# Attention rows stored with g alone and their norms beside them; the readers multiply

## Chip, cores, metric

One core of a Trainium2 chip runs the whole program. The metric is the device time of one execution in microseconds (us).

## What is computed

```python
# attention, 8 batches, 8 heads, 576 rows, 64 columns a head
kv  = einsum('bhsd,bhse->bhde', k, v)
out = einsum('bhsd,bhde->bhse', q, kv)
x   = out / sqrt(mean(out * out, -1) + 1e-6) * g_norm      # -> x [4608, 512]
# one of 8 experts for each row whose skip score is above 0; the others pass
e   = argmax(x @ w_gate); p = softmax(x @ w_gate)[e]
x   = x + p * (maximum(x @ w1[e], 0) @ w2[e])              # 512 -> 1024 -> 512
# dense part, all rows
h   = x @ w_in                                             # 512 -> 2048
y   = (h * sigmoid(h)) @ w_out                             # 2048 -> 512
```

## The kernel before, in words

Three stages follow each other: attention with the routing of its rows (0 to about 138 us in the trace), the eight experts (147 to 418 us), the dense part (418 us to the end).

**Attention.** The loop runs over batches b = 0 to 7 and, inside, over units u of four heads and two 128-row tiles (u = 0 to 3); an odd batch has a fifth unit, the 64 rows left over of each of two batches (`attend_rest`). Tiles of one pair of batches are numbered 0 to 8, so a pair has 9 x 8 = 72 norms a partition. `attend` of a unit stands one unit behind the rest of the loop (`prev`). For each unit (`attend_main`, L448) TensorE writes po (L458) in PSUM, which holds for each head 64 output columns and 9 scores (the skip score and 8 gate logits, not yet normed). ScalarE squares the 64 columns into sq (L477) and copies them into the rows tile in SBUF (L484). VectorE copies the 9 scores into sc (L485) and sums the squares into ssq (L487). In two units of batch 6 ScalarE makes the sums itself (`sums_by_act`, L472). In batch 7 VectorE multiplies by g while it copies (`g_early`, L480).

`norm` (L601) takes ssq and makes inv, one over the root, with ten small VectorE operations (L607 to L627) on mh and tmp in SBUF, once for each batch and in two parts for batch 7. `scale` (L638) then multiplies each row tile on GpSimd, by inv and by g, two operations a tile; `scale_inv` does it for batch 7's last tiles on ScalarE (L653, eight operations) and VectorE (L648). `routing` works on sc times inv (L697) and gives each row its expert, its gate weight and its place.

`store` writes a batch's rows to `xs` in DRAM. A row there has 4 pieces of XQ = 129 floats: 128 columns and the gate weight. `STORES` says at which batch and unit each store is issued on SP's queue; batches 6 and 7 are stored behind the loop. `weave` puts the operations of several generators alternately into an engine's order; beside that the order is the order of the program text.

**Experts.** While expert u runs, the rows of expert u + 1 are gathered (L990, GpSimd's queue), three tiles of up to 128 rows, named xe_0 to xe_2. An expert has 8 steps f; a step is 12 matmuls into ph (`first`, L1325), the two halves of h by ScalarE (L1331) and VectorE (L1332), and 9 matmuls of the step before into acc (`second`, L1377). In the last steps of an expert TensorE transposes the next expert's rows into pt (L1226), and ScalarE and VectorE copy them as high and low halves xT (L1237, L1238). Weights arrive as f32 and are split into high and low halves: w by ScalarE and VectorE (L186, L187). Some pieces of the dense weights go through a longer split: five VectorE operations (L197 to L209), one of ScalarE, two GpSimd multiplies and subtractions (L221, L222), and a VectorE sum (L217) that waits for L222. Each engine takes its own instructions strictly in order.

**Dense part.** Groups of rows are read by place (`fetch_blocks`, L1024); for each tile VectorE transposes blocks (L1259, and L1288 in `operand_parts`) and the operands are made for TensorE.

## Time and profile before

| | |
|---|---|
| median of 3 runs (lowest to highest) | 1189.66 us (1189.15 to 1190.32) |
| the profiled execution, its own time | 1186.21 us |
| its span in the trace | 1184.4 us |
| mean granted TensorE clock | 0.962 of full speed |
| busy: TensorE, its weight loads, VectorE, ScalarE, GpSimd | 95%, 78%, 52%, 39%, 31% of the span |
| chain that ended last | PE 84%, DVE 7%, DMA 3%, issue 2%, ACT 1%, POOL 1% |
| costliest lines | TensorE L1377 278.7 us, L1325 269.4 us, L1520 265.1 us |

PE is TensorE, DVE VectorE, ACT ScalarE, POOL GpSimd, SP SyncE. A busy share over the whole span mixes the three stages; a stage has to be read from a window of its own. The chain goes back from the last instruction, at each step to what released it.

### The profile page before, as it was taken

To read this page: it belongs to the slowest core of one execution; us is meant where nothing else is said; L and a number is where in the kernel's file an instruction comes from. 1 tells how busy PE (TensorE), PEld (TensorE's weight loads), DVE (VectorE), ACT (ScalarE), POOL (GpSimd) and SP (SyncE) were. 2 spreads that over 40 slices of the span, in tenths; PEclk is the share of its full clock that TensorE was granted. 3 is DMA by queue.
4 is the path that set the end of the run, shared out by engine and by line. 5 is a ranking of instruction groups with operands and counts; after the bars stand their busy time and mean duration, and the time that the engine had idled before them with its cause. 6 is when DMAs were issued, how large, how long until landed. Compare 5 with 4: busy or idle time off the path is not lost.

```text
span 1184.4 us, 18142 instructions
## 1 busy us (share of the span) xinstructions
PE 1119.5 (95%) x6991; PEld 929.4 (78%) x6991; DVE 615.7 (52%) x1217; ACT 467.3 (39%) x877; POOL 361.8 (31%) x360
## 2 busy tenths in 40 slices
PE   7785299999999899999999999999999999999998
PEld 6674298888887788888888888888888888888886
DVE  2679867778788667643544622355222453223222
ACT  2444244444455433432433444433244432344221
POOL 2668435444444347233053324120043200000000
PEclk8787599999999899999999999999999999999999
DMA  9956656666766624058651376532566422654202
GB/s 337 358 227 254 213 174 204 207 203 201 218 219 220 214 85 156 1 180 282 202 157 56 129 267 211 180 125 85 192 214 217 145 107 103 218 186 173 103 36 71
DMA packets 65272, 211.16 MB, mean 178 GB/s; under 512 B 9840, under 2 KB 24688, under 8 KB 53024
## 3 DMA queue, kind: packets, MB, share of 16 engines
q1 hardware_dynamic: 55760, 189.44, 46.2%
q0 software_dynamic: 8064, 20.48, 5.9%
q8 instruction: 56, 0.92, 0.3%
q10 hardware_dynamic: 1360, 0.05, 0.1%
q14 instruction: 32, 0.26, 0.1%
HBM read 162.67 MB, written 47.27 MB: 177 GB/s over the span
## 4 chain that ended last, share of the span: by engine, by line
PE 84%; DVE 7%; DMA 3%; issue 2%; ACT 1%; POOL 1%; SPq 0%; POOLq 0%; ACTq 0%; another core or an unknown queue 0%; DVEq 0%
PE acc L1520 22%; PE acc L1377 19%; PE ph L1325 19%; PE pa L1473 11%; PE pc L1473 6%; PE pb L1473 3%; DMA v<-in_v_dram 1%; PE pt L1226 1%; PE kv L417 1%; PE po L458 1%; DVE ssq L487 1%; DVE w L187 1%; POOL x L222 0%; DVE scratch L699 0%; PE G L438 0%
## 5 line engine op out<-in xcount | busy, mean ns | idle before, releaser
L1377 PE MATMUL acc<-w,h 128*128 128x512 f32 x1128 | 278.7, 393 | 3.0 <-DVE xe L1387 1.8
L1325 PE MATMUL ph<-xT,w 128*128 128x512 f32 (+7 forms) x1344 | 269.4, 350 | 1.2 <-DVE w L187 1.2
L1520 PE MATMUL acc<-entry,h 128*128 128x512 f32 x1152 | 265.1, 392 | 0.0
L1520 PEld LDWEIGHTS acc<-entry,h 128*128 128x128 f32 x1152 | 216.3, 188 | 47.9
L1325 PEld LDWEIGHTS ph<-xT,w 128*128 128x128 f32 x1344 | 228.6, 192 | 31.1 <-DVE w L187 1.4
L1377 PEld LDWEIGHTS acc<-w,h 128*128 128x128 f32 x1128 | 202.1, 182 | 50.6 <-DVE xe L1387 2.1
L1024 POOL DMA_INDIRECT x<-xs,qidx x128 | 128.3, 1002 | 113.9 <-DVE room L1288 48.8
L1501 DVE TENSOR_TENSOR h<-g,h 128x512 fp32r<-128x512 f32 x96 | 66.5, 693 | 147.9 <-ACT h L1500 147.9
L1473 PE MATMUL pa<-b,entry 128*128 128x512 f32 x576 | 141.8, 393 | 0.0
L1473 PEld LDWEIGHTS pa<-b,entry 128*128 128x128 f32 x576 | 108.2, 188 | 24.8
L1500 ACT ACTIVATE h<-g 128x512 fp32r<-128x512 f32 x96 | 60.5, 630 | 146.6 <-PE acc L1520 146.6
L1339 DVE TENSOR_TENSOR h<-sg,h 128x512 fp32r<-128x512 f32 x48 | 34.8, 724 | 107.5 <-ACT h L1338 107.5
L187 DVE TENSOR_TENSOR w<-stg_None,w 128x1024 fp32r<-128x1024 f32 x64 | 80.2, 1255 | 17.9 <-ACT w L186 17.6
L1455 ACT ACTIVATE g<-g 128x512 f32<-128x512 f32 x72 | 45.4, 633 | 103.3 <-DVE g L1453 103.3
L1337 ACT ACTIVATE sg<-ph 128x512 f32<-128x512 f32 x48 | 28.6, 597 | 128.2 <-PE ph L1325 128.2
L221 POOL TENSOR_TENSOR x<-x,x 128x512 f32<-128x512 f32 x32 | 41.5, 1298 | 113.9 <-DVE x L209 109.1
L1473 PE MATMUL pc<-b,entry 128*128 128x512 f32 x288 | 74.3, 393 | 0.0
L1331 ACT ACTIVATE h<-ph 128x304 fp32r<-128x304 f32 (+6 forms) x64 | 27.9, 436 | 112.0 <-PE ph L1325 108.9
L186 ACT ACTIVATE w<-stg_None 128x1024 fp32r<-128x1024 f32 x64 | 67.1, 1050 | 9.0 <-DMA xs<-rows 8.6
L1473 PEld LDWEIGHTS pc<-b,entry 128*128 128x128 f32 x288 | 54.1, 188 | 12.4
L222 POOL TENSOR_TENSOR x<-x,w 128x512 f32<-128x512 f32 x32 | 62.9, 1967 | 0.8 <-ACT w L220 0.8
L1453 DVE TENSOR_TENSOR g<-pc,u 128x512 f32<-128x512 f32 x24 | 16.6, 692 | 73.0 <-PE pc L1473 73.0
(219 smaller groups left out, 1143.6 us busy)
## 6 DMA issues: line engine op xcount, KB each, us to landing
entry<-wa SPq DMA_DIRECT2D x42, 1024.0 KB, 4.8
stg_None<-in_we_dram SPq DMA_DIRECT2D x64, 512.0 KB, 3.6
entry<-wb SPq DMA_DIRECT2D x24, 1024.0 KB, 4.8
stg<-in_wf_dram SPq DMA_DIRECT2D x32, 512.0 KB, 4.1
xs<-rows SPq DMA_DIRECT2D x8, 1032.0 KB, 8.8
wb<-w SPq DMA_DIRECT2D x16, 512.0 KB, 4.9
wa<-parts SPq DMA_DIRECT2D x32, 256.0 KB, 4.1
k<-in_k_dram SPq DMA_DIRECT2D x7, 1024.0 KB, 7.8
```

The lines of the kernel that those rows point to most:

```text
L186: nc.scalar.activation(w[:, 0, :], t.bitcast(F32), AF.Copy)
L187: nc.vector.tensor_tensor(w[:, 1, :], t.bitcast(F32), w[:, 0, :].bitcast(F32), ALU.subtract)
L221: nc.gpsimd.tensor_tensor(x3, x3, x2, ALU.mult)
L222: nc.gpsimd.tensor_tensor(x1, x1, w[:, 0, :].bitcast(F32), ALU.subtract)
L1024: nc.gpsimd.indirect_dma_start(out=rows_of[u][s][:, a * XQ:(a + 1) * XQ], out_offset=None, in_=xblocks, in_offset=bass.IndirectOffsetOnAxi ...
L1325: nc.tensor.matmul(ph[:, 0:n], w[:, wi, kk * P:(kk + 1) * P], x[:, xi, 0:n], start=(kk == 0 and a == 0), stop=(kk == KD - 1 and a == 2),)
L1377: nc.tensor.matmul(accs[u, s][0:m], h[:, hi, s * P:s * P + m], w[:, wi, DM:2 * DM], start=(f == 0 and a == 0), stop=(last and a == 2),)
L1455: nc.scalar.activation(g, acc, AF.Silu)
L1473: nc.tensor.matmul(p, w[:, wi, kk], x[:, xi, kk], start=(i in FIRST_IN_BANK and kk == 0 and a == 0), stop=(kk == 1 and a == 2), skip_group ...
L1500: nc.scalar.activation(h[:, 0], g, AF.Copy)
L1501: nc.vector.tensor_tensor(h[:, 1], g, h[:, 0].bitcast(F32), ALU.subtract)
L1520: nc.tensor.matmul(acc[ni, s], h[:, hi, s * P:(s + 1) * P], w[:, wi], start=(j == 0 and fi == 0 and a == 0), stop=(last and a == 2),)
```

## The change

Rows in `xs` become four pieces of 131 floats (128 columns, the gate weight, two norms), and are stored with g multiplied in but without the norm. Whoever reads a row multiplies its columns by the norms first (`scale_row`), and sets the norms to 1 where the row is written back and read again. `norm` runs once for two batches (for batches 6 and 7 singly), twelve operations on 72 (32, 40) columns whose intermediate results lie partly in PSUM, and ScalarE writes its result into the rows (L632). ScalarE copies the scores (L486, L510). GpSimd keeps the multiply by g, now issued behind each pair of units. Line numbers move by some lines: L1332, L187, L217, L221, L222, L1226 and L1238 are L1323, L197, L227, L231, L232, L1215 and L1227 in the changed kernel. TensorE's instructions stand in the same order.

```diff
-    XQ = P + 1
+    XQ = P + 3
...
+    def norm_of(row):
+        return row.rearrange("p (a w) -> p a w", w=XQ)[:, :, P + 1:XQ]
+    def scale_row(row, on):
+        xv = x_of(row).rearrange("p a (j d) -> p a j d", j=2)
+        on.tensor_tensor(xv, xv, norm_of(row).unsqueeze(3).to_broadcast(list(xv.shape)), ALU.mult)
...
         def g_early(b, r):
-            return b == B - 1
-        def sums_by_act(b, u):
-            return (b, u) in ((B - 2, 1), (B - 2, 2))
+            return b == B - 1 and r >= 2
...
-            nc.vector.tensor_copy(sc[:, ts, hs, :], pv[:, :, :, D:DC])
-            if not sums_by_act(b, 2 * r2 + hh):
-                nc.vector.tensor_reduce(ssq[:, ts, hs], sq, AX.X, ALU.add)
+            nc.scalar.activation(sc[:, ts, hs, :], pv[:, :, :, D:DC], AF.Copy)
+            nc.vector.tensor_reduce(ssq[:, ts, hs], sq, AX.X, ALU.add)
...
-        def norm(b, part_=None):
+        def norm(*bs):
...
+            r0, r1, r2 = (root[:, k, 0:n] for k in range(3))
...
+            vec.scalar_tensor_tensor(y, rest, 1.5, r0, ALU.add, ALU.mult)
+            for b in bs:
+                i, k = tiles_of(b)
+                to = rows_b[b][:, 0:k - i].rearrange("p t (a w) -> p t a w", w=XQ)[:, :, :, P + 1:XQ]
+                nc.scalar.activation(to, inv[:, i:k].rearrange("p t (a j) o -> p t a (j o)", j=2), AF.Copy)
+            yield
...
-                for i in parts:
-                    f = (inv[:, t].rearrange("p (a j) o -> p a j o", j=2), grow[:, None, None, :])[i]
-                    nc.gpsimd.tensor_tensor(xv, xv, f.to_broadcast([P, HP, 2, D]), ALU.mult)
+                nc.gpsimd.tensor_tensor(xv, xv, grow[:, None, None, :].to_broadcast([P, HP, 2, D]), ALU.mult)
...
-        STORES = {(6, 3): (0, 1, 2, 3), (7, 1): (4,), (7, 4): (5,)}
+        STORES = {(4, 3): (0, 1), (6, 3): (2, 3), (7, 1): (4,), (7, 3): (5,)}
...
-                if u == 0 and b >= 1:
-                    todo = [norm(b - 1)]
+                if u == 0 and b >= 2:
+                    todo = [norm(b - 2, b - 1)] if b % 2 == 0 else []
+                    if b == B - 1:
+                        todo.append(norm(b - 1))
...
-                    weave(norm(B - 1, (0, 2)))
-                    scale(B - 1, (0, 1), (0,))
...
-        weave(norm(B - 1, (2, R + 1)))
-        scale(B - 1, (2,), (0,))
-        weave(scale_inv(B - 1, (3,)))
+        weave(norm(B - 1))
...
+    def scale_rows(u, s, on):
+        row = rows_of[u][s][0:tokens_of[u][s]]
+        scale_row(row, on)
+        if u < E:
+            nc.vector.memset(norm_of(row), 1.0)
...
+        scale_row(rows_of[u][s], nc.vector)
         t = xgp.tile([P, XW], F32, tag="xg", name="turned")[:, 0:DM]
...
         for v, t in ((u, ta), (u + 1, tb)):
+            scale_row(rows_of[v][s], vec)
             vec.transpose(t.rearrange("p (k a i) -> p a k i", k=KD, a=KQ), x_of(rows_of[v][s]))
...
     for s in range(len(tokens_of[0])):
+        scale_rows(0, s, nc.vector)
...
+        if now is not None and nxt <= E and 0 <= f - 2 < len(tokens_of[nxt]):
+            scale_rows(nxt, f - 2, nc.gpsimd)
```

VectorE in expert 3, about step 4, before (h is `first`'s output, w and x are pieces of weights, xT the turned rows of the next expert):

```order
L1332 SCALAR_TENSOR_TENSOR h<-ph,h 128x320 [waits Activation_49]
L187 TENSOR_TENSOR w_3713<-stg_None,w_3713 128x1024 [waits DMAHW6_49,Activation_49]
L1332 SCALAR_TENSOR_TENSOR h<-ph,h 128x320 [waits Activation_49]
L217 TENSOR_TENSOR w_3516<-x_3674,x_3675 128x512 [waits Pool_49]
L187 TENSOR_TENSOR w_3744<-stg_None,w_3744 128x1024 [waits DMAHW7_49,Activation_49]
```

and with the change (xe_1 is the second row tile of the next expert; L1323, L197 and L227 are L1332, L187 and L217 of before):

```order
L1206 MEMSET xe_0_3538 128x4x2 [waits DMASW5_49,DMASW2_49,Pool_49]
L1323 SCALAR_TENSOR_TENSOR h<-ph,h 128x320 [waits Activation_49]
L197 TENSOR_TENSOR w_3654<-stg_None,w_3654 128x1024 [waits DMAHW6_49,Activation_49]
L1206 MEMSET xe_1_3540 128x4x2 [waits DMASW6_49,DMASW3_49,Pool_49]
L1323 SCALAR_TENSOR_TENSOR h<-ph,h 128x320 [waits Activation_49]
L227 TENSOR_TENSOR w_3455<-x_3613,x_3614 128x512
L197 TENSOR_TENSOR w_3687<-stg_None,w_3687 128x1024 [waits DMAHW7_49,Activation_49]
```

A memset of the second row tile's norms now stands between L197 and the second h, and waits for GpSimd; the sum L227 no longer has a wait of its own.

GpSimd at the same place, before (the gathers, then two splits):

```order
L990 DMA xe_0_3599<-xs,gidx 128x516 [waits DMASW2_49,PE_49]
L990 DMA xe_1_3601<-xs,gidx 128x516 [waits DMASW3_49,PE_49]
L990 DMA xe_2_3603<-xs,gidx 48x516 [waits DMASW7_49,DMASW4_49,PE_49]
L221 TENSOR_TENSOR x_3675<-x_3675,x_3676 128x512 [waits DVE_49,Activation_49]
L222 TENSOR_TENSOR x_3674<-x_3674,w_3516 128x512 [waits Activation_49,Pool_49]
L221 TENSOR_TENSOR x_3751<-x_3751,x_3752 128x512 [waits DVE_49,Activation_49]
L222 TENSOR_TENSOR x_3750<-x_3750,w_3749 128x512 [waits Activation_49]
```

and with the change:

```order
L970 DMA xe_0_3538<-xs,gidx 128x524 [waits DMASW2_49,PE_49]
L970 DMA xe_1_3540<-xs,gidx 128x524 [waits DMASW3_49,PE_49]
L970 DMA xe_2_3542<-xs,gidx 48x524 [waits DMASW4_49,PE_49]
L79 TENSOR_TENSOR xe_0_3538<-xe_0_3538 128x4x128 [waits DMASW5_49]
L231 TENSOR_TENSOR x_3614<-x_3614,x_3615 128x512 [waits DVE_49,Activation_49]
L232 TENSOR_TENSOR x_3613<-x_3613,w_3455 128x512 [waits Activation_49,Pool_49]
L79 TENSOR_TENSOR xe_1_3540<-xe_1_3540 128x4x128 [waits DMASW6_49]
L79 TENSOR_TENSOR xe_2_3542<-xe_2_3542 48x4x128 [waits DMASW7_49]
```

The multiply of row tile 0 stands between the gathers and the split's L231; those of tiles 1 and 2 stand behind L232, tile 1's being the one for which VectorE's second memset waits.

ScalarE where batch 6 begins, before (rows5 and rows6 are the rows of batches 5 and 6):

```order
L502 ACTIVATE sq<-po 128x2x4x64 [waits DVE_49,PE_49]
L509 ACTIVATE rows_1341<-po 128x2x4x64
L477 ACTIVATE sq<-po 128x512 [waits DVE_49,PE_49]
L484 ACTIVATE rows_1580<-po 128x2x2x128
L423 ACTIVATE kvT_1701<-kv_1626 128x256 [waits PE_49]
L472 ACTIVATE sq,ssq_1582<-po 128x64 [waits DVE_49,PE_49,Activation_49]
```

and with the change:

```order
L502 ACTIVATE sq<-po 128x2x4x64 [waits DVE_49,PE_49]
L509 ACTIVATE rows_1309<-po 128x2x4x64
L510 ACTIVATE sc_1100<-po 128x2x4x9
L632 ACTIVATE rows_1099<-inv_1101 128x16x2 [waits DVE_49]
L632 ACTIVATE rows_1309<-inv_1101 128x20x2
L478 ACTIVATE sq<-po 128x512 [waits PE_49]
```

The copy of the scores and two writes of norms, which wait for VectorE's norm, now stand ahead of the square of batch 6's first unit.

## Rows read from the trace of the kernel before

**Rows 1.** Windows in attention: busy PE, PEld, DVE, ACT, POOL; clock, DMA share, GB/s.
```profile
75.00:90.00 15.00, 13.22 (x336) 11.82 (x340) 13.30 (x45) 7.79 (x18) 11.10 (x11) 0.68 0.46 176
...
sum 60.00, PE 29.93 PEld 26.14 DVE 55.08 ACT 22.52 POOL 40.58; mean PE 7.48 PEld 6.53 DVE 13.77 ACT 5.63 POOL 10.15
```

**Rows 2.** Windows of 20 us: one inside an expert, one in the dense part.
```profile
260.00:280.00 20.00, 20.00 (x109) 16.50 (x108) 15.57 (x24) 10.49 (x17) 9.33 (x9) 1.00 0.80 249
600.00:620.00 20.00, 20.00 (x90) 16.56 (x89) 6.79 (x13) 5.97 (x10) 14.88 (x14) 1.00 0.61 182
```

**Rows 3.** Timeline of VectorE while GpSimd scales rows, 92 to 96 us.
```profile
92.48 1.20 DVE L607 TENSOR_SCALAR mh<-ssq 128x40 f32<-128x40 f32 x1
...
94.93 1.06 DVE L615 TENSOR_TENSOR tmp<-inv 128x40 f32<-128x40 f32 x1
```

**Rows 4.** Timeline of VectorE in batch 7, 113.5 to 120 us.
```profile
113.20 0.41 DVE L480 TENSOR_TENSOR rows<-po,grow 128x256 f32<-128x256 f32 x1
113.53 0.22 DVE L485 COPY sc<-po 128x72 f32<-128x72 f32 x1
113.67 0.67 DVE L487 TENSOR_REDUCE ssq<-sq 128x8 f32<-128x512 f32 x1
...
118.83 0.17 DVE L623 TENSOR_TENSOR tmp<-inv 128x16 f32<-128x16 f32 x1
119.04 0.17 DVE L625 SCALAR_TENSOR_TENSOR tmp<-tmp,mh 128x16 f32<-128x16 f32 x1
```

**Rows 5.** Windows of one tile or line alone, 60 to 140 us: L609 to L627, L607, L485.
```profile
60.00:140.00 80.00, 15.96 (x54) 0.69 0.65 240
...
60.00:140.00 80.00, 3.98 (x6) 0.69 0.65 240
...
71.00:138.00 67.00, 3.56 (x16) 0.65 0.67 248
```

**Rows 6.** Groups by line, 60 to 140 us, VectorE and then ScalarE.
```profile
L711 DVE TENSOR_TENSOR scratch<-scratch,mx 128x72 f32<-128x72 f32 (+2 forms) x4 | 0.8, 212 | 0.0
...
L648 DVE TENSOR_TENSOR rows<-rows,inv 128x512 f32<-128x512 f32 x1 | 0.7, 681 | 0.0
...
L477 ACT ACTIVATE sq<-po 128x512 f32<-128x512 f32 x17 | 10.2, 598 | 14.6 <-PE po L458 14.5
...
L720 ACT ACTIVATE es<-ls 128x72 f32<-128x72 f32 (+2 forms) x4 | 1.0, 244 | 10.8 <-DVE ls L709 10.8
```

**Rows 7.** Timelines of VectorE and TensorE at expert 0's start.
```profile
144.31 2.35 DVE L187 TENSOR_TENSOR w<-stg_None,w 128x1024 fp32r<-128x1024 f32 x2
...
147.27 1.11 PE L1226 MATMUL pt<-ident,xe 128*128 128x128 f32 x4 [1.35 <-DMA xe<-xs,gidx]
```

**Rows 8.** Timelines in expert 3, step 4: VectorE, GpSimd, TensorE.
```profile
272.46 0.49 DVE L1332 SCALAR_TENSOR_TENSOR h<-ph,h 128x320 fp32r<-128x320 f32 x1 [0.31 <-ACT h L1331]
273.35 0.69 DVE L217 TENSOR_TENSOR w<-x,x 128x512 fp32r<-128x512 f32 x1 [0.39 <-POOL x L222]
...
277.81 0.47 DVE L1238 TENSOR_TENSOR xT<-pt,xT 128x304 fp32r<-128x304 f32 x1
...
271.05 2.27 POOL L222 TENSOR_TENSOR x<-x,w 128x512 f32<-128x512 f32 x1
...
278.26 1.13 PE L1226 MATMUL pt<-ident,xe 128*128 128x128 f32 x6
```

**Rows 9.** Groups by line of GpSimd, 71 to 138 us.
```profile
L638 POOL TENSOR_TENSOR rows<-rows,inv 128x512 f32<-128x512 f32 x21 | 22.3, 1066 | 17.8 <-DVE inv L627 11.3 <-DVE sc L485 6.6
```

**Rows 10.** TensorE's timeline around a stall in expert 1, and windows just behind it.
```profile
203.69 2.17 PE L1325 MATMUL ph<-xT,w 128*128 128x352 f32 x12
...
210.42 0.51 PE L1226 MATMUL pt<-ident,xe 128*128 128x128 f32 x3 [2.17 <-DVE xT L1238]
210.73 3.69 PE L1325 MATMUL ph<-xT,w 128*128 128x352 f32 x12
...
212.00:214.00 2.00, 2.00 (x9) 2.00 (x8) 1.30 (x3) 0.00 (x0) 1.61 (x1) 0.50 0.40 78
```

More of the change, by code (lines that the diff above doesn't have):

```diff
@@ L78, in tile_kernel @@
     qidx = const.tile([P, KQ, NTILE], I32, name="qidx")
-    quad = const.tile([P, 1], F32, name="quad")
+    few = const.tile([P, 2], F32, name="few")
+    quad = few[:, 0:1]
     NP = GT + -(-CAPS[E - 1] // P)
-    mine = const.tile([P, NP, 2], I32, name="mine")
-    goes = const.tile([P, NP], I32, name="goes")
-    inew = const.tile([P, NP, 2], I32, name="inew")
+    moves = const.tile([P, 5 * NP], I32, name="moves")
+    mine, inew = (moves[:, 2 * NP * i:2 * NP * (i + 1)].rearrange("p (t c) -> p t c", c=2) for i in range(2))
+    goes = moves[:, 4 * NP:5 * NP]
     perm = tc.dram_tile([NP * P, 2], I32, name="perm")
@@ L103, in tile_kernel @@
     NPL = 3
-    paced = const.tile([1, 1], F32, name="paced")
+    paced = few[0:1, 1:2]
     NEA = NB // 4
@@ L400, in tile_kernel @@
         }
+        held["ssum"] = held["tl"][:, :, 0:1]
+        root = held["coh"].rearrange("p t e c -> p (t e c)").rearrange("p (k n) -> p k n", k=3)
+        ssq_all = in_psum([TP, H])
         Aall = ac.tile([P, NTILE, E], BF16, name="Aall")
@@ L592, in tiles_of @@
             return (R, TP) if b % 2 else (0, R)
-        def norm(b, part_=None):
+        def norm(*bs):
             vec = nc.vector
-            t0, t1 = tiles_of(b)
-            if part_:
-                t0, t1 = t0 + part_[0], t0 + part_[1]
+            t0, t1 = tiles_of(bs[0])[0], tiles_of(bs[-1])[1]
             n = (t1 - t0) * H
-            _, ssq, inv = scores[b // 2]
-            sq = ssq[:, t0:t1].rearrange("p t h -> p (t h)")
+            inv = scores[bs[0] // 2][1]
+            sq = ssq_all[:, t0:t1].rearrange("p t h -> p (t h)")
@@ L605, in norm @@
             y = inv[:, t0:t1].rearrange("p t h o -> p (t h o)")
-            mh, tmp = (arem.tile([P, TP * H], F32, tag=nm, name=nm)[:, 0:n] for nm in ("mh", "tmp"))
-            vec.tensor_scalar(mh, sq, -0.5 / D / 2.25, -0.5e-6 / 2.25, ALU.mult, ALU.add)
+            r0, r1, r2 = (root[:, k, 0:n] for k in range(3))
+            mh, tmp, rest = (arem.tile([P, TP * H], F32, tag=nm, name=nm)[:, 0:n] for nm in ("mh", "tmp", "rest"))
+            vec.tensor_scalar(r0, sq, -0.5 / D / 2.25, -0.5e-6 / 2.25, ALU.mult, ALU.add)
@@ L622, in norm @@
             yield
-            vec.tensor_tensor(tmp, y, y, ALU.mult)
+            vec.tensor_tensor(tmp, r1, rest, ALU.mult)
             yield
-            vec.scalar_tensor_tensor(tmp, tmp, 2.25, mh, ALU.mult, ALU.mult)
+            vec.scalar_tensor_tensor(r0, tmp, 1.25, r2, ALU.add, ALU.mult)
             yield
-            vec.scalar_tensor_tensor(y, tmp, 1.5, y, ALU.add, ALU.mult)
+            vec.scalar_tensor_tensor(tmp, r0, 2.25, mh, ALU.mult, ALU.mult)
             yield
-        def scale(b, tiles, parts=(0, 1)):
-            inv = scores[b // 2][2]
+            vec.tensor_tensor(rest, r0, tmp, ALU.mult)
@@ L674, in routing @@
             j0 = g * TP + t0
-            sc, _, inv = scores[g]
+            sc, inv = scores[g]
             sc, inv = sc[:, t0:t1], inv[:, t0:t1]
@@ L853, in attend @@
             qT = kvq[b][2][:, u] if u < 4 else rems["q", b // 2]
-            sc, ssq, _ = scores[b // 2]
+            sc, _ = scores[b // 2]
             t0 = R * (b % 2)
-            args = rows_b[b], sc[:, t0:t0 + R + 1], ssq[:, t0:t0 + R + 1]
+            args = rows_b[b], sc[:, t0:t0 + R + 1], ssq_all[:, t0:t0 + R + 1]
             if u < 4:
@@ L860, in attend @@
                 attend_rest(b, qT, *args)
+            if u % 2 or u == R:
+                scale(b, [r for r in ((R,) if u == R else (u - 1, u)) if not g_early(b, r)])
             if u == 3 and b + 2 < B:
@@ L1093, in tile_kernel @@
             gather(row, go)
+            scale_row(row, vec)
+            vec.memset(norm_of(row), 1.0)
             ge = oc.tile([P, E], F32, name="ge")
@@ L1128, in tile_kernel @@
             vec.scalar_tensor_tensor(
-                x_of(row), py.rearrange("p (a w) -> p a w", a=KQ), row[:, P:XQ], x_of(row), ALU.mult, ALU.add
+                x_of(row), py.rearrange("p (a w) -> p a w", a=KQ), row[:, P:P + 1], x_of(row), ALU.mult, ALU.add
             )
```

52 lines of the change are left out of this document (13 added, 39 removed).

## The prediction

> **What bounds the kernel now.** I read windows first, because the busy share over the whole span mixes three stages. In attention's later part, 75 to 135 us, VectorE is busy 55.08 of 60 us while TensorE has 29.93 [rows 1]: there VectorE sets the pace, except between 75 and 90 us, where TensorE (13.22 of 15) is as full as VectorE (13.30). From the experts on TensorE is busy 20.00 of 20 us, beside a VectorE at 15.57 in an expert and 6.79 in the dense part [rows 2]. So an instruction saved on VectorE is worth its time in attention and nothing in the dense part, and in the experts VectorE has a quarter of its time free, but not always where it is needed.
>
> Then I read VectorE's timeline for operations longer than their size explains. A norm operation on a few columns takes 0.17 us [rows 4]; the same lines take 1.20 and 1.06 us while GpSimd scales rows [rows 3]. The multiply by inv on GpSimd takes 1066 ns [rows 9], so such an operation waits about as long as one GpSimd multiply.
>
> **Attention: what goes.** From 60 to 140 us there are six norms of ten operations: 15.96 us in L609 to L627 and 3.98 in L607 [rows 5], 19.9 us of VectorE, where 60 operations of 0.17 to 0.20 us would be about 11. In their place stand four norms of twelve, two of them 72 wide (batches 2 and 3, 4 and 5), two 32 and 40 wide. No row shows the new form; the nearest is a 72-wide operation in PSUM, 212 ns [rows 6]. 24 x 0.212 + 24 x 0.20 = 9.9 us. Of two dependent operations the second starts 0.21 us after the first, which is busy for 0.17 [rows 4], so twelve operations fewer also save 12 x 0.04 = 0.5 us. Together -10.5 us.
>
> The 16 score copies between 71 and 138 us are busy 3.56 us [rows 5], but the operation behind a copy starts 0.14 us after it (113.53 to 113.67), and the copy 0.33 us after the multiply by g [rows 4]. So copies give 16 x 0.14 = -2.2 us, and the four multiplies by g that leave batch 7's first two units 4 x 0.33 = -1.3. L648 goes: -0.7 [rows 6]. Two units of batch 6 get their sum of squares back on VectorE: 2 x 0.67 = +1.3 [rows 4]. VectorE has 13.4 us less to do.
>
> **Attention: what is added.** The norms are written into the rows by ScalarE, in front of the next unit's square. While they wait for VectorE's norm, that square waits too, and behind the norm VectorE finds no sq to sum. The price of one such place is two short writes and a square, 2 x 0.244 + 0.598 = 1.1 us [rows 6]. It comes at the start of batches 4 and 6, and with one write in batch 7: 3.0 us. ScalarE's copies of scores lie in ScalarE's free time (22.52 of 60 us busy [rows 1]); if that cover were gone they would cost up to 0.24 us a unit.
>
> 13.4 - 3.0 = 10.4 us; VectorE is the limit for 55.08 / 60 of the time, which leaves 9.6. In batch 5 (75 to 90 us) TensorE takes over as the limit, so I take off the 2 us or so by which the stalled norm there is shortened. **-7.5 us.** Bounds: -10.5 if nothing is taken off, -5 if TensorE and ScalarE become the limit in batches 4 and 6 as well. The stores issued earlier and rows 1.6% longer (131 for 129 floats) move data that the wait at the end does not see, except batch 7's own store, whose 1.6% is under 0.2 us.
>
> **Expert 0's start.** Three multiplies on VectorE are put ahead of the copies of the turned rows. Before, TensorE gets the last row tile at 147.27 us, waiting for its gather; VectorE has two L187 until 146.66 [rows 7]. The three multiplies stand behind those: 146.66 + 3 x 0.68 = 148.7 us, with L648's duration for a 128x512 multiply [rows 6]. **+1.4 us** (0.7 if the first fits in earlier, 2.0 with the memsets).
>
> **Experts 1 to 7: where I expect the change to lose.** The GpSimd multiplies themselves are cheap: 3 x 1.07 = 3.2 us in an expert of 33 us, on an engine that is busy 9.33 of 20 us [rows 2, 9]. What matters is the memset of a row's norms, on VectorE, which waits for the multiply. In the order, the second memset stands before h of step 4, and its multiply stands on GpSimd behind L222.
>
> In expert 3, L222 runs from 271.05 us for 2.27, to 273.32 [rows 8]. The multiply then ends at 274.39, so h, which started at 272.46, starts 1.9 us later. L217, which waited for L222 until 273.35, follows h of 0.49 us: 274.9, or 1.55 us later than before; if it is held by the third multiply (until 275.45), 2.1. I take 2.0, because L222 beside VectorE takes 2.27 us and norm operations beside GpSimd were held for a multiply's length [rows 3, 8]: the two do not run side by side. Behind L217, L187 and five split operations follow without a gap up to xT, which started at 277.81 and ended at 278.28. TensorE wants it for the second half of its six transposes, at about 278.26 + 1.13 / 2 = 278.83 [rows 8]. The slack is 0.55 us, the stall 1.45. In expert 1 there is no slack at all: TensorE already waits there 2.17 us for xT [rows 10]. With a mean slack of 0.3 us, 7 x 1.7 = **+11.9 us**. Bounds: 0, if VectorE makes the delay good, and 7 x 2.1 = 14.7 with no slack. The first memset, ahead of h of step 3, waits for the gather and its own multiply; VectorE had idle time behind that h, and I cost it at nothing.
>
> **The dense part.** 32 multiplies of 0.68 us are 22 us of VectorE over some 760 us, where it is two thirds idle and TensorE never waits [rows 2]: 0. If one of them came late, TensorE would show a wait at L1473, where it has none now.
>
> **Sum.** -7.5 + 1.4 + 11.9 = +5.8 us. The profiled execution took 1186.21 us with a span of 1184.4; its steps carry over to the median, 1189.66, which is 0.3% higher: 1195.5 us.
>
> **A rule against the change.** The rows say that one of the two engines is held [rows 3]. The Trainium skill, GPSIMD Engine Reference, section Specifications, says that GpSimd shares its SBUF interfaces with VectorE and that they contend when VectorE's instruction is in a 2-port mode or has two SBUF inputs; and SBUF - State Buffer, section Terms, that the loser is blocked for the whole instruction. By that rule L217 and L187, with two SBUF inputs each, would lose the whole third multiply as well, 0.55 us more than the lower figure of 1.55 for each expert, which is already the upper one above; the sum would be 7 x 0.1 = 0.7 us higher. The rows agree as far as the stalled norm operations go; that both engines lose in turn is open.
>
> **Rivals.**
>
> *The multiplies stay hidden.* GpSimd has half its time free; VectorE is idle for 1.5 us about step 4 (0.31 and 0.39 of it in front of rows shown [rows 8]) and may take the delay there, or the multiply of tile 1 may come before L222 is due. It decides if the delay of xT stays under the slack of 0.55 us. Then -7.5 + 1.4 = -6.1: 1183.6 us, faster. Against it: the order puts the multiply behind L222 and a VectorE memset behind the multiply.
>
> *Half of it.* Where L222 no longer runs beside L187, because VectorE waits, it would take 1.3 us and not 2.27, and the delay would be halved: +6 in place of +11.9, and the whole about +0.
>
> *The clock falls as well.* After the stall of 2.17 us in expert 1, the window from 212 to 214 us has a granted clock of 0.50, TensorE's lower level, and twelve matmuls took 3.69 us where the same twelve had taken 2.17 [rows 10]: 1.5 us. If each of six more stalls does that, +9: 1204.5 us. It needs stalls near 2 us; 1.5 may not do.
>
> **How the numbers follow.** Chances: forecast 0.48, hidden 0.20, half 0.17, clock 0.15. Under 0.2% (2.4 us) a measurement of this kernel can't be told from no change. Hidden gives faster; half lies on both sides of no change (0.06 faster, 0.08 same, 0.03 slower); the forecast's bounds (attention -10.5 with small stalls) give 0.02 same. Faster 0.26, same 0.10, slower 0.64. Range: from the hidden case, 1183, to the clock's, 1205; the forecast alone has 1191 to 1200.
>
> **What would show it.** In the new trace: norm operations of 0.2 us with no 1 us stalls; attention's last store some 7 us earlier; a VectorE wait at the memset (L1206) for GpSimd's L79 in each of experts 0 to 6, and TensorE waits of 1 to 2 us at the transposes, for xT; dense windows full. If TensorE's waits in the experts stay near those of before, the forecast is wrong and the hidden case right.

## The result, and the profile after

The changed kernel takes 1202.42 us (median of 5 runs, 1197.08 to 1205.12) where the kernel before takes 1189.15 beside it (5 runs, 1187.67 to 1190.32): 1.0108 times the time, 95% interval 1.0081 to 1.0135, or 10 to 16 us more. Forecast were 1195.5 us, 5.8 more, in a range of 1183 to 1205. On a second chip, where both kernels were run again, the ratio was 1.0147 (1.0131 to 1.0164).

The profiled execution is the slowest of the five, 1205.12 us with a span of 1203.3, and that of the kernel before (1186.21) was faster than any of its five, so the pair shows the loss at its largest: 18.9 us more span. On the second chip it is the other way round: the change's trace is of its fastest execution (1204.03 us, median 1214.01), and the two spans differ by 9.2 us where the medians differ by 17.5. The other 8 us stand in no trace. Four marks cut both traces into stages: the first gather for expert 0, the first matmul into ph, the start of the last accumulate of expert 7, the end.

| us | before | change | before, second chip | change, second chip |
|---|---|---|---|---|
| attention and routing, to the first gather | 139.99 | 139.65 | 142.19 | 137.65 |
| from there to the first matmul | 8.33 | 11.21 | 8.27 | 11.21 |
| the eight experts | 275.27 | 291.36 | 275.61 | 289.16 |
| from there to the end | 760.8 | 761.1 | 767.0 | 764.3 |

The loss is in the experts, 16.1 and 13.6 us, with 2.9 at their start. Attention gives back 0.3 and 4.5. The part behind the experts differs by +0.3 and -2.7.

**Attention.** The first of the four windows from 75 to 135 us and their sum, as in [rows 1], of the change (the columns are those named there):

```profile
75.00:90.00 15.00, 13.67 (x285) 12.35 (x285) 9.10 (x27) 6.21 (x16) 3.64 (x4) 0.50 0.81 304
...
sum 60.00, PE 34.05 PEld 30.54 DVE 45.60 ACT 21.86 POOL 16.26; mean PE 8.51 PEld 7.63 DVE 11.40 ACT 5.46 POOL 4.06
```

In these 60 us VectorE's busy time falls from 55.08 to 45.60, by 9.5 us (on the second chip from 55.03 to 49.32, by 5.7). Up to the first gather, earlier batches included, it falls from 92.76 to 79.12, by 13.6. But TensorE's rises from 29.93 to 34.05, and its clock in the first window is 0.50, the lower level, where it was 0.68. That clock belongs to this execution: the six other traces of kernels with the same attention have 0.66 to 0.77 there, and their first gather comes at 135.18 to 137.88 us. What VectorE does with the time it saves is in its waits for ScalarE, 60 to 140 us (us in sum, times, longest), the kernel before and then the change:

```profile
DVE sc L485 <- ACT rows L484: 6.8, 7, 2.6
```

```profile
DVE scratch L487 <- ACT sq L478: 16.9, 11, 3.2
```

and ScalarE's waits, the change, same stretch:

```profile
ACT rows L632 <- DVE inv L628: 14.2, 4, 4.2
ACT sq L478 <- PE po L467: 10.9, 10, 4.9
```

VectorE waits 16.9 us for squares, and ScalarE in turn for TensorE's po, and 14.2 us in front of the writes of norms.

**Start of expert 0**, timelines of VectorE, GpSimd and TensorE, to compare with [rows 7]:

```profile
144.36 2.35 DVE L197 TENSOR_TENSOR w<-stg_None,w 128x1024 fp32r<-128x1024 f32 x2
146.62 1.42 DVE L79 TENSOR_TENSOR xe<-xe 128x512 f32<-128x512 f32 x2
...
148.09 1.66 DVE L79 TENSOR_TENSOR xe<-xe 128x512 f32<-128x512 f32 x1
...
148.13 1.06 POOL L79 TENSOR_TENSOR xe<-xe 128x512 f32<-128x512 f32 x1
...
147.37 1.97 PE L1215 MATMUL pt<-ident,xe 128*128 128x128 f32 x8 [4.25 <-DVE xe L79]
149.80 1.11 PE L1215 MATMUL pt<-ident,xe 128*128 128x128 f32 x4 [0.47 <-DVE xe L79]
```

TensorE's transposes begin at 147.37, since row tiles 0 and 1 too are multiplied only behind the two weight splits. The third multiply takes 1.66 us, where L648 took 0.68 [rows 6]: a GpSimd multiply runs beside it. In the kernel with unscaled rows (see the experiments) no GpSimd multiply stands there, and the third takes:

```profile
146.22 0.68 DVE L79 TENSOR_TENSOR xe<-xe 128x512 f32<-128x512 f32 x1
```

**Experts.** GpSimd, VectorE and TensorE in expert 3 around step 4, to compare with [rows 8]:

```profile
276.51 1.36 POOL L79 TENSOR_TENSOR xe<-xe 128x512 f32<-128x512 f32 x1 [2.27 <-DMA xe<-xs,gidx]
278.30 1.30 POOL L231 TENSOR_TENSOR x<-x,x 128x512 f32<-128x512 f32 x1 [0.43 <-DVE xe L1206]
279.56 2.28 POOL L232 TENSOR_TENSOR x<-x,w 128x512 f32<-128x512 f32 x1
281.80 2.04 POOL L79 TENSOR_TENSOR xe<-xe 128x512 f32<-128x512 f32 x2
...
278.61 2.07 DVE L197 TENSOR_TENSOR w<-stg_None,w 128x1024 fp32r<-128x1024 f32 x1
282.89 0.48 DVE L1323 SCALAR_TENSOR_TENSOR h<-ph,h 128x320 fp32r<-128x320 f32 x1 [2.21 <-issue]
...
283.29 1.10 DVE L227 TENSOR_TENSOR w<-x,x 128x512 fp32r<-128x512 f32 x1
...
288.17 0.46 DVE L1227 TENSOR_TENSOR xT<-pt,xT 128x304 fp32r<-128x304 f32 x1
...
281.62 0.27 PE L1215 MATMUL pt<-ident,xe 128*128 128x128 f32 x1
282.89 0.33 PE L1215 MATMUL pt<-ident,xe 128*128 128x128 f32 x1 [1.00 <-POOL xe L79]
283.89 0.26 PE L1215 MATMUL pt<-ident,xe 48*128 48x48 f32 x1 [0.66 <-POOL xe L79]
284.08 2.02 PE L1316 MATMUL ph<-xT,w 128*128 128x320 f32 x12
```

In the kernel before, the same three transposes stand together and wait for nothing:

```profile
273.82 0.57 PE L1226 MATMUL pt<-ident,xe 128*128 128x128 f32 x3
```

GpSimd's L232 ends at 281.84 and the multiplies of row tiles 1 and 2 follow, to 283.84. TensorE turns tile 0 at 281.62, waits 1.00 us for tile 1, turns it, waits 0.66 us for tile 2. VectorE's h of step 4 starts at 282.89, when the first of these multiplies is over, and xT at 288.17. TensorE's waits in the experts, summed, the change and then the kernel before:

```profile
PE pt L1215 <- POOL xe L79: 11.7, 12, 2.1
PE pt L1215 <- DVE xT L1227: 2.1, 2, 1.1
```

```profile
PE pt L1226 <- DVE xT L1238: 4.0, 3, 2.2
```

There were 4.0 us of waits for xT and none for a multiply before. The whole of the eight experts, one window (us; then busy us of TensorE, its loads, VectorE, ScalarE, GpSimd; clock), the change:

```profile
150.86:442.22 291.36, 274.00 (x1441) 231.30 (x1441) 220.01 (x346) 130.83 (x210) 142.34 (x112) 0.96 0.58 186
```

and the kernel before:

```profile
148.32:423.59 275.27, 266.98 (x1441) 227.52 (x1441) 209.74 (x326) 130.42 (x210) 115.64 (x89) 0.97 0.63 200
```

The 1441 matmul records are the same. TensorE stands still for 291.36 - 274.00 = 17.4 us against 8.3, 9.1 more, and is busy 7.0 us longer with the same work. On the second chip the two parts are 8.8 and 4.7.

Part of the longer busy time is the clock. The stretches of the experts in which it was at 0.50, summed, are 150.86 to 155.90, 210.60 to 214.00, 248.10 to 251.50, 319.80 to 323.20, 357.40 to 360.80 and 412.00 to 418.80 us in the change, and 148.32 to 152.90, 210.90 to 214.30 and 395.30 to 402.10 in the kernel before:

```profile
sum 25.44, PE 24.04 PEld 21.86 DVE 22.07 ACT 7.37 POOL 4.73; mean PE 4.01 PEld 3.64 DVE 3.68 ACT 1.23 POOL 0.79
```

```profile
sum 14.78, PE 14.05 PEld 13.17 DVE 9.70 ACT 4.31 POOL 6.29; mean PE 4.68 PEld 4.39 DVE 3.23 ACT 1.44 POOL 2.10
```

TensorE is busy 10.0 us longer at the lower level. Twelve matmuls took 3.67 us there and 2.17 at the upper level (rows of expert 1 below), so 1.50 of 3.67 us are lost, and the 10.0 us cost about 4.1, an estimate. On the second chip it is 18.06 us against 14.01, or about 1.7. What is left, 2.9 and 3.1 us, is alike on both chips. Most of it is transposes that run one by one: 0.27 + 0.33 + 0.26 = 0.86 us in expert 3 where 0.57 stood before, so by estimate 2.0 us in seven experts.

Windows of 2 us behind the waits of expert 3 and of expert 4:

```profile
284.00:286.00 2.00, 2.00 (x14) 1.95 (x15) 1.97 (x4) 0.43 (x1) 0.00 (x0) 1.00 0.00 0
320.00:322.00 2.00, 2.00 (x8) 1.91 (x9) 1.97 (x4) 0.42 (x1) 0.00 (x0) 0.50 0.00 0
```

and TensorE's timeline in expert 4:

```profile
318.92 0.33 PE L1215 MATMUL pt<-ident,xe 128*128 128x128 f32 x1 [1.42 <-POOL xe L79]
319.92 0.34 PE L1215 MATMUL pt<-ident,xe 48*128 48x48 f32 x1 [0.67 <-POOL xe L79]
320.19 3.30 PE L1316 MATMUL ph<-xT,w 128*128 128x304 f32 x12
```

Behind waits of 1.00 and 0.66 us the clock stays at 1.00; behind 1.42 and 0.67 it falls to 0.50, and twelve matmuls take 3.30 us, where expert 3's, slightly larger, take 2.02 (284.08 us). But the length of the waits does not decide it. In expert 1 they are 2.09 and 0.67 us on both chips; TensorE on the first and on the second:

```profile
210.56 0.39 PE L1215 MATMUL pt<-ident,xe 80*128 80x80 f32 x1 [0.67 <-POOL xe L79]
210.68 3.67 PE L1316 MATMUL ph<-xT,w 128*128 128x352 f32 x12
```

```profile
207.46 0.29 PE L1215 MATMUL pt<-ident,xe 80*128 80x80 f32 x1 [0.67 <-POOL xe L79]
207.54 2.17 PE L1316 MATMUL ph<-xT,w 128*128 128x352 f32 x12
```

The granted clock behind them is 0.50 on the first chip and 1.00 on the second. In these two traces of the first chip TensorE waits for nothing in the dense part.

### The profile page after: what moved, and what is told of

It is laid out like the page before. It is cut to its first block, busy times and chain, and to the rows that moved or that the text cites. A ratio compares the mean times of both kernels' runs of the same rounds, so it can differ in the third digit from the quotient of the medians.

```text
span 1203.3 us, 18138 instructions
## 1 busy us (share of the span) xinstructions
PE 1131.7 (94%) x6991; PEld 938.9 (78%) x6991; DVE 636.4 (53%) x1206; ACT 470.5 (39%) x885; POOL 357.5 (30%) x352
## 4 chain that ended last, share of the span: by engine, by line
PE 77%; DVE 5%; POOL 3%; issue 2%; DMA 1%; ACT 1%; ACTq 0%; POOLq 0%; DVEq 0%
PE acc L1511 22%; PE ph L1316 18%; PE acc L1368 17%; PE pa L1464 11%; PE pc L1464 6%; PE pb L1464 3%; DVE w L197 2%; POOL x L232 1%; POOL xe L79 1%; PE pt L1215 1%; ACT w L196 1%; DVE x L215 1%; DVE x L209 1%; DMA xe<-xs,gidx 1%; POOL x L231 0%
## 5 line engine op out<-in xcount | busy, mean ns | idle before, releaser
L1316 PEld LDWEIGHTS ph<-xT,w 128*128 128x128 f32 x1344 | 231.3, 194 | 30.7 <-DVE w L197 1.0
L197 DVE TENSOR_TENSOR w<-stg_None,w 128x1024 fp32r<-128x1024 f32 x64 | 85.6, 1338 | 13.8 <-ACT w L196 13.5
L1328 ACT ACTIVATE sg<-ph 128x512 f32<-128x512 f32 x48 | 28.6, 596 | 118.3 <-PE ph L1316 118.3
L231 POOL TENSOR_TENSOR x<-x,x 128x512 f32<-128x512 f32 x32 | 42.0, 1312 | 101.2 <-DVE x L219 59.8
L232 POOL TENSOR_TENSOR x<-x,w 128x512 f32<-128x512 f32 x32 | 61.8, 1932 | 0.8 <-ACT w L230 0.8
L639 POOL TENSOR_TENSOR rows<-rows,grow 128x512 f32<-128x512 f32 x33 | 38.4, 1189 | 78.3 <-ACT rows L485 78.3
```

What stands on the lines that cost most here:

```text
L197: nc.vector.tensor_tensor(w[:, 1, :], t.bitcast(F32), w[:, 0, :].bitcast(F32), ALU.subtract)
L231: nc.gpsimd.tensor_tensor(x3, x3, x2, ALU.mult)
L232: nc.gpsimd.tensor_tensor(x1, x1, w[:, 0, :].bitcast(F32), ALU.subtract)
L1316: nc.tensor.matmul(ph[:, 0:n], w[:, wi, kk * P:(kk + 1) * P], x[:, xi, 0:n], start=(kk == 0 and a == 0), stop=(kk == KD - 1 and a == 2),)
```

## Experiments

Three chips carry these runs: one the unscaled rows, the memset, the multiplies ahead and the stores; another both kernels again, VectorE at the same places and the norm writes (the second chip of the table above); a third the rest. On which chip the first pair ran is not on record. A ratio is always to runs of the kernel before on the same chip. That kernel took 1204, 1196 and 1197 us there, so absolute times of different chips aren't compared. "Experts" is the length between the second and the third mark of the table above, from the trace, "idle" is that less TensorE's busy time.

The part behind the experts has a spread of its own. In every trace of these three chips ScalarE stands still there, in front of one line (L1328 of the change, L1337 of the kernel before), for 19.5 to 35.2 us in sum, with no releaser in the program that the trace names, in the kernel before too (23.7); in the first pair it never does. That part takes 764 to 785 us in these traces and 761 in the first pair. So an edit in the experts is judged by their length, and small differences of the whole are not placed. Whether the dense part's multiplies cost something isn't shown beyond the two pairs of the first table, which differ there by +0.3 and -2.7 us.

| kernel | ratio (95%) | experts | TensorE busy | idle |
|---|---|---|---|---|
| before, again | 0.9994 (0.9978 to 1.001) | 275.61 | 266.82 | 8.8 |
| change, again | 1.0147 (1.0131 to 1.0164) | 289.16 | 271.56 | 17.6 |
| experts' rows unscaled | 0.9998 (0.9976 to 1.002) | 270.55 | 262.84 | 7.7 |
| memset on GpSimd | 1.0228 (1.0187 to 1.027) | 293.89 | 274.54 | 19.4 |
| multiplies ahead, GpSimd | 1.0132 (1.0077 to 1.0187) | 288.47 | 270.26 | 18.2 |
| multiplies on VectorE, same places | 1.0414 (1.0377 to 1.0451) | 316.21 | 277.55 | 38.7 |
| multiplies on VectorE, ahead | 1.0074 (1.0046 to 1.0101) | 281.52 | 267.21 | 14.3 |
| stores as before | 1.0145 (1.0107 to 1.0183) | 291.59 | 274.30 | 17.3 |
| norm writes on GpSimd | 1.0105 (1.0065 to 1.0145) | 290.50 | 273.14 | 17.4 |
| scores by ScalarE alone | 0.9976 (0.9954 to 0.9998) | 270.53 | 262.57 | 8.0 |
| attention's part alone, rows whole | 0.9963 (0.9943 to 0.9983) | 272.07 | 264.14 | 7.9 |

**Both kernels again.**

> The kernel before, unchanged, for a trace on the same chip as the three runs beside it. Ratio 1.00; expert 0's first matmul into ph near 148 us and the last accumulate of expert 7 near 424 us, as in the trace already read.

> The change, unchanged, beside the others. If the loss is a property of the kernel and not of one chip: ratio 1.008 to 1.014, TensorE's 12 waits for L79 again 10 to 14 us in sum.

The loss is the kernel's, not one chip's: 1.0147, a little over what was expected, and TensorE waits 11.5 us for L79 in twelve waits, as on the first chip. The kernel before starts and ends its experts 2 us later than expected, at 150.46 and 426.07 us.

**What do the readers' multiplies cost in experts 1 to 7?**

```diff
-        if now is not None and nxt <= E and 0 <= f - 2 < len(tokens_of[nxt]):
+        if now is not None and nxt == E and 0 <= f - 2 < len(tokens_of[nxt]):
             scale_rows(nxt, f - 2, nc.gpsimd)
```

> Leaves out the multiply by the norms, and the memset, of the rows of experts 1 to 7 (expert 0 and the dense part keep theirs). Theory A (the readers' multiplies cost nearly all of the loss: TensorE waits for them, and its clock drops behind some of the waits): TensorE's 12 waits for L79 go, experts take the time of before, and the whole comes to 1188 to 1192 us. Rival B (longer rows in DRAM, or attention, cost it): no more than 4 us gained, over 1197.

Experts 1 to 7 then compute on rows without their norms, so this kernel only prices the multiplies. The window of the eight experts:

```profile
148.26:418.81 270.55, 262.84 (x1441) 223.27 (x1441) 212.36 (x325) 130.52 (x210) 122.46 (x93) 0.99 0.63 201
```

Theory A holds: the waits for L79 in the experts are gone, TensorE stands still for 7.7 us and not 17.4, and the whole takes the time of before (ratio 0.9998; the 1188 to 1192 us of the expectation don't apply to this chip, where the kernel before takes 1204). The multiplies in experts 1 to 7 therefore carry the loss, 18.6 to 20.8 us of experts by the two traces of the change, and 21.0 by the kernel with the stores as before, which ran on the same chip (291.59 us). Longer rows, expert 0 and the dense part together cost what attention gives, to within the interval of some 2.5 us either way.

**Who waits for the multiply: VectorE at its memset, or TensorE?**

```diff
-            nc.vector.memset(norm_of(row), 1.0)
+            on.memset(norm_of(row), 1.0)
```

> The memset of a row's norms is done by GpSimd behind its multiply, so VectorE waits for no multiply. Theory A (TensorE itself waits for the multiplies of row tiles 1 and 2, which stand behind L232): TensorE's waits for L79 stay at 9 to 13 us and the time at 1196 to 1204. Rival C (the step of the forecast: VectorE is held by its memset and hands xT over late): the waits fall below 4 us and the time to 1188 to 1194.

TensorE's waits, 138 to 440 us:

```profile
PE pt L1215 <- POOL xe L79: 14.4, 12, 2.1
...
PE pt L1215 <- DVE xT L1227: 1.5, 2, 1.0
```

With no memset of VectorE in front of h, TensorE still waits for the multiplies, 14.4 us in twelve waits. Rival C, the step on which the forecast was built, falls: in expert 3 h of step 4 starts at 278.17 us, as soon as L197 is done, and TensorE waits all the same. The waits are longer than expected: behind tile 2's multiply mostly 1.12 us instead of 0.67. In expert 3 a GpSimd memset of 0.11 us stands in front of that multiply, which itself takes 1.33 us beside VectorE's L227. The experts are 2.3 us longer than with the stores as before on the same chip; why the whole is longer by more than that isn't shown.

**Multiplies ahead of the split, on GpSimd.**

```diff
-        if now is not None and nxt <= E and 0 <= f - 2 < len(tokens_of[nxt]):
+        if now is not None and nxt < E and f == 2:
+            for s in range(len(tokens_of[nxt])):
+                scale_row(rows_of[nxt][s][0:tokens_of[nxt][s]], nc.gpsimd)
+        if now is not None and nxt < E and f == 4:
+            for s in range(len(tokens_of[nxt])):
+                nc.vector.memset(norm_of(rows_of[nxt][s][0:tokens_of[nxt][s]]), 1.0)
+        if now is not None and nxt == E and 0 <= f - 2 < len(tokens_of[nxt]):
             scale_rows(nxt, f - 2, nc.gpsimd)
```

> GpSimd's three multiplies of experts 1 to 7 stand together, ahead of the split's L231 and L232; the memsets stand one or two steps later on VectorE. Theory A: the multiplies end before TensorE's transposes, the waits for L79 fall below 2 us, and the time to 1188 to 1193 (1 to 3 us of it lost again where L227 now waits longer for L232). Rival D (GpSimd beside VectorE slows both, whatever the order): the waits move to xT or w, and the time stays above 1196.

TensorE's waits, same stretch:

```profile
PE pt L1215 <- DVE xT L1227: 13.0, 7, 3.2
...
PE ph L1316 <- DVE w L197: 2.1, 4, 1.1
```

The waits for L79 in the experts are gone, as theory A said, and 13.0 us of waits for xT have come in their place, which it put at 1 to 3. L231 and L232 now follow three multiplies on GpSimd, L227 on VectorE waits for L232, and xT stands behind L227. VectorE, same stretch, and one of its splits in expert 3:

```profile
DVE w L227 <- POOL x L232: 10.5, 5, 3.7
```

```profile
275.62 4.30 DVE L197 TENSOR_TENSOR w<-stg_None,w 128x1024 fp32r<-128x1024 f32 x1 [0.79 <-ACT w L196]
```

In experts 1, 4, 5 and 6 L227 waits for L232. In experts 2 and 3 it doesn't; there L197 takes 4.03 and 4.30 us beside GpSimd's multiplies, where 1.2 is its usual time. So the time theory A gave is wrong, and rival D is right that the waits move to xT: in part by the longer chain through GpSimd, in part by the two engines slowing each other.

**On VectorE instead.** First at the same places of the program:

```diff
-            scale_rows(nxt, f - 2, nc.gpsimd)
+            scale_rows(nxt, f - 2, nc.vector if nxt < E else nc.gpsimd)
```

> The multiplies of experts 1 to 7 on VectorE, at the places where the memsets stand. Theory A2 (the loss is the chain through GpSimd: a row's multiply behind L232, or L227 behind L232 behind the multiplies, with VectorE waiting for either): no wait is left between the engines, two multiplies of 0.7 us fit nearly into the idle time around step 4, experts take 271 to 277 us from the first matmul to the last accumulate, where the change has 291, and the whole is 0 to 4 us over the kernel before. Rival G (the work itself is what is too much, wherever it is done): VectorE hands xT over 1.4 us late in each expert, 10 us lost, experts at 283 or more.

Timelines of VectorE, GpSimd and TensorE in expert 3:

```profile
286.11 0.69 DVE L79 TENSOR_TENSOR xe<-xe 128x512 f32<-128x512 f32 x1
...
288.95 1.78 DVE L79 TENSOR_TENSOR xe<-xe 128x512 f32<-128x512 f32 x1
...
295.63 0.68 DVE L79 TENSOR_TENSOR xe<-xe 48x512 f32<-48x512 f32 x1
...
287.91 2.27 POOL L232 TENSOR_TENSOR x<-x,w 128x512 f32<-128x512 f32 x1
...
296.36 0.34 PE L1215 MATMUL pt<-ident,xe 48*128 48x48 f32 x1 [5.24 <-DVE xe L79]
```

Theory A2 was wrong, and rival G's bound holds for another reason than the one it gave: 316 us of experts, with TensorE waiting 37.3 us for L79 itself and 1.1 for xT. Row tile 2's multiply (295.63) stands behind the five operations of a split, and TensorE waits 5.24 us for it. That was open to be read from the order beforehand. Second, tiles 1 and 2 together ahead of h:

```diff
-        if now is not None and nxt <= E and 0 <= f - 2 < len(tokens_of[nxt]):
+        if now is not None and nxt < E and f in (2, 3):
+            for s in range(len(tokens_of[nxt])):
+                if min(s, 1) == f - 2:
+                    scale_rows(nxt, s, nc.vector)
+        if now is not None and nxt == E and 0 <= f - 2 < len(tokens_of[nxt]):
             scale_rows(nxt, f - 2, nc.gpsimd)
```

> As e4_multiplies_on_vector, but the multiplies of row tiles 1 and 2 stand together ahead of h of step 4 and of the split's five operations. Theory L (in e4 TensorE waited 37 us for VectorE because row tile 2's multiply stood behind those five operations): TensorE's waits for L79 fall below 5 us; what is left are waits for xT of 1 to 2 us in an expert, experts take 278 to 288 us, ratio 1.004 to 1.011, at or below the change itself. Rival M (VectorE and GpSimd hold each other up): experts at 290 us or more.

TensorE's waits, 138 to 450 us:

```profile
PE pt L1215 <- DVE xe L79: 8.7, 9, 4.3
PE pt L1215 <- DVE xT L1227: 6.2, 8, 1.1
```

The place was what mattered: 281.5 us of experts, waits for L79 of 8.7 us of which 4.3 are one wait at expert 0's start, waits for xT 6.2. Theory L holds: without that one wait, of which the change has the like, the waits for L79 are 4.4 us. This is the best place tried for multiplies in the experts by the experts' length, and by the middle of the interval it still costs 0.7%; the interval (1.0046 to 1.0101) overlaps that of the change on the first chip (1.0081 to 1.0135).

**Attention: the early stores.** Batches 0 and 1 stored in batch 6 again:

```diff
-        STORES = {(4, 3): (0, 1), (6, 3): (2, 3), (7, 1): (4,), (7, 3): (5,)}
+        STORES = {(6, 3): (0, 1, 2, 3), (7, 1): (4,), (7, 3): (5,)}
```

> Only the stores of batches 0 and 1 go back from batch 4 to batch 6, where the kernel before has them. Theory E (the early stores share the DMA engines with the last loads of k and v, TensorE waits for those, and stays at its lower clock from 76 to 92 us): the clock of 75 to 90 us rises from 0.50 to about 0.7 and expert 0 starts 3 to 6 us earlier, the whole at 1196 to 1199. Rival F (attention is bound by ScalarE and TensorE now, whatever the stores do): less than 1.5 us earlier.

Theory E falls: the first gather is issued at 138.81 us, no earlier than in the three kernels beside it with early stores (136.73 to 137.88), and their clock from 75 to 90 us is 0.66 to 0.77, not 0.50, against 0.66 here. The ratio, 1.0145, is that of the change on the second chip.

**Attention: ScalarE's waits for the norms.**

```diff
-                nc.scalar.activation(to, inv[:, i:k].rearrange("p t (a j) o -> p t a (j o)", j=2), AF.Copy)
+                nc.gpsimd.tensor_copy(to, inv[:, i:k].rearrange("p t (a j) o -> p t a (j o)", j=2))
```

> Only the writes of the norms into the rows (L632) move from ScalarE to GpSimd. Theory H (in attention ScalarE stands in front of these writes, 14.2 us in four places, with the next unit's square behind them, and VectorE then waits for that square): the four waits go, VectorE's waits for sq fall by 3 us or more, expert 0 starts 2 to 4 us earlier. Rival I (TensorE's clock and its inputs set attention's pace): expert 0 starts less than 1 us earlier.

VectorE's waits, 60 to 140 us:

```profile
DVE scratch L487 <- ACT sq L478: 11.4, 7, 2.7
```

ScalarE's four waits for the norm go, and VectorE's wait for squares falls from 13.9 us (the change on the same chip) to 11.4, short of the 3 us that theory H said. The first matmul into ph starts at 146.70 us, the change's on that chip at 148.86: 2.2 us earlier, at the lower end of what theory H said. Some of this can be chance: the kernel with multiplies on VectorE has the change's attention and issues its first gather on that chip at 136.82 us, the change at 137.65 and this one at 135.46. The ratios, 1.0105 and 1.0147, have intervals that overlap (1.0065 to 1.0145, 1.0131 to 1.0164), so a gain in the whole is likely and not shown.

**The change's parts that don't touch the readers.** One alone, in the kernel before:

```diff
-            nc.vector.tensor_copy(sc[:, ts, hs, :], pv[:, :, :, D:DC])
+            nc.scalar.activation(sc[:, ts, hs, :], pv[:, :, :, D:DC], AF.Copy)
...
-            nc.vector.tensor_copy(sc[:, R].rearrange("p (a j) c -> p j a c", j=2), pv[:, :, :, D:DC])
+            nc.scalar.activation(sc[:, R].rearrange("p (a j) c -> p j a c", j=2), pv[:, :, :, D:DC], AF.Copy)
```

> The kernel before with one part of the change alone: ScalarE, not VectorE, copies the scores. Theory (VectorE has 16 copies of 0.14 us less in the stretch where it sets the pace): 1 to 3 us faster, ratio 0.998 to 0.999. Rival (ScalarE's chain of square, rows and scores frees po later, and TensorE and VectorE wait for that): no change or slower, ratio 1.000 to 1.003.

0.9976 (0.9954 to 0.9998): 2.9 us faster by the middle of the interval, at the upper end of the theory; the interval reaches from 0.2 to 5.5 us. No trace of the kernel before stands beside it on that chip, so where the gain lies isn't shown. And all of attention's part, with the multiply by inv in attention:

```diff
-    XQ = P + 3
+    XQ = P + 1
...
             for b in bs:
-                i, k = tiles_of(b)
-                to = rows_b[b][:, 0:k - i].rearrange("p t (a w) -> p t a w", w=XQ)[:, :, :, P + 1:XQ]
-                nc.scalar.activation(to, inv[:, i:k].rearrange("p t (a j) o -> p t a (j o)", j=2), AF.Copy)
+                if b < B - 1:
+                    for r in range(tiles_of(b)[1] - tiles_of(b)[0]):
+                        scale_inv(b, r, "pool")
...
         weave(norm(B - 1))
+        scale_inv(B - 1, 0, "pool")
+        scale_inv(B - 1, 1, "pool")
+        scale_inv(B - 1, 2, "act")
...
         weave(weigh)
+        scale_inv(B - 1, 3, "vec")
+        scale_inv(B - 1, 4, "vec")
...
-        scale_rows(0, s, nc.vector)
...
-            scale_rows(nxt, f - 2, nc.gpsimd)
```

> The attention part of the change (norm once for two batches in PSUM, scores copied by ScalarE, early stores), but the rows are multiplied by their norms in attention, by GpSimd, and for batch 7 by all three engines; the readers multiply nothing and rows keep 129 floats. Theory J (attention's part of the change is a gain by itself, GpSimd's second multiply lies in its free time): TensorE's waits and the length of the experts as in the kernel before (275 us from first matmul to last accumulate, or 271), expert 0 starts 1 to 4 us earlier, the whole 2 to 6 us below the kernel before, ratio 0.995 to 0.998. Rival K (VectorE stalls beside GpSimd's multiplies in the new norm as it did in the old one): expert 0 no earlier than before, ratio 1.000 or above.

TensorE's waits for xT, 138 to 450 us, and the window of the eight experts:

```profile
PE pt L1216 <- DVE xT L1228: 3.7, 3, 2.3
```

```profile
146.71:418.78 272.07, 264.14 (x1441) 224.41 (x1441) 209.93 (x326) 130.57 (x210) 116.55 (x90) 0.99 0.63 203
```

Theory J holds in the whole and in the experts: 0.9963 (0.9943 to 0.9983), 2.0 to 6.8 us faster than the kernel before in twelve runs; the earlier start of expert 0 can't be read without a trace of the kernel before on that chip. This version beats both kernels. The experts are those of the kernel before, with no multiply in them, and attention keeps the new norm. How much the new norm adds to the score copies alone isn't shown: the two intervals overlap (0.9943 to 0.9983, 0.9954 to 0.9998), and expert 0's first matmul starts at 146.71 us here and at 145.81 with the scores alone, on the same chip.

## Why the prediction came out as it did

The sign and the place were right: attention gains a little, the experts lose more. The sum was less than half of what was measured, 5.8 us where the medians differ by 13.3 on the first chip and 17.5 on the second, and both large terms were off, both towards a faster kernel. That 1202.42 lies in the range is luck in part: the forecast alone reached to 1200, and the bound of 1205 came from a rival, the clock, of which only a part came true.

**Attention, -7.5 us: the step that failed most.** What was to leave VectorE left it: the old norms were 19.9 us busy from 60 to 140 us, the new ones are 48 operations of about 0.21, 10.3 us (forecast 9.9), and none stalls beside GpSimd: the longest take 0.24 us. (The prediction speaks of the same lines in [rows 3] and [rows 4]; they are different lines, but L611 at 94.71 us, between the two long ones, took 0.18, so the reading holds.) VectorE's busy time from 75 to 135 us fell by 9.5 us. The step that failed is the next one: that VectorE stays the limit for 55.08 / 60 of the time once it is relieved, with 2 us taken off for batch 5 alone. It did not stay the limit: it waits 16.9 us for squares (13.9 on the second chip), where it had waited 6.8 (9.0) for ScalarE's rows, and ScalarE in turn waits for TensorE and for the norm. The norm writes account for 2.5 us of these waits (norm writes on GpSimd); what holds the rest is not shown. The gain was 0.3 us on one chip and 4.5 on another, by single traces; the last store is issued at 132.62 us and not 133.05, where the prediction looked for some 7 us. The 0.3 is of the one execution whose clock was 0.50 from 75 to 90 us. The lower bound, -5, was the better value. The price of a norm write in front of a square, 1.1 us, was fair: at batch 4 VectorE idles 0.91 us there, and the 2.5 us stand against 3.0 for the three places.

**Expert 0's start, +1.4 us:** +2.9. The cause was right, the term mis-sized. I priced the third multiply at 0.68 us, which took 1.66 beside a GpSimd multiply and ended at 149.75 us instead of 148.7. Where no GpSimd multiply stands there (the rows unscaled), expert 0's first matmul comes 10.48 us behind the first gather and not 11.21, so this is 0.7 of the 1.5 us. The rest is that TensorE waits for all three tiles, and I let only the last one wait: in that kernel its twelve transposes run from 145.50 us to the first matmul without a gap.

**Experts, +11.9 us:** 16.1 and 13.6. What was right is the origin, GpSimd's multiplies of tiles 1 and 2 behind L232, at each of seven experts. The mechanism, a VectorE memset that makes xT late, was not the one that counted: TensorE's transposes of the same rows wait for these multiplies directly, 11.7 us in twelve waits, and went on waiting when the memset was taken off VectorE. The waits for xT that the prediction named as its sign fell from 4.0 to 2.1 us; that its 11.9 came near is luck in part, since both paths start at the same late multiply. xT is late as well, but behind the transposes. In idle time the term is 9.1 us, less than forecast, because the waits for xT of before shrink. The rest is 7.0 and 4.7 us of longer busy time with the same matmuls. Of it about 4.1 and 1.7 us are the rival I had set apart, a lower clock behind some of the waits, given 9 us and a chance of 0.15 as an alternative; it came along with the forecast's waits, at less than half its price, and it did not need a stall near 2 us: in expert 2 waits of 0.79 and 0.67 went before it. Of the remaining 3 us nothing stood in the prediction: by estimate 2.0 are transposes that run one by one.

**Dense part, 0:** right by the two pairs of traces, +0.3 and -2.7 us; in the first pair TensorE has no wait there.

**The rule on the shared interfaces.** L79 of 1.66 us on VectorE beside a GpSimd multiply, L197 of 2.07 at 278.61 beside L231 and L232 and of 1.21 at 284.31 beside none, GpSimd's L232 of 2.28 beside L197 and of 1.26 at 207.25 us with VectorE idle: the rows show that either engine can be the one that is held. That the two contend when VectorE's instruction has two SBUF inputs is what the Trainium skill, GPSIMD Engine Reference, section Specifications, states, and the trace agrees. The 0.55 us that the prediction let L217 lose by that rule came in part: L227, which is L217's new line, took 1.10 us beside the third multiply (283.29) and 0.69 before [rows 8]. The delay it adds is in the waits above, not on top of them.

**The other rivals.** That the multiplies stay hidden is refuted by the waits. Half of the loss through a shorter L232 is too: L232 took 2.28 us, as before.
